# Output banks that alternate between groups, first loads in another order, and three copies done by DMA, in an attention and MLP kernel

## The chip, the cores and the metric

One core of a Trainium2 chip runs the kernel. The number is device time in microseconds, median of several runs. Before the change it is 1764.37 us, the median of three runs (1763.39 to 1766.12).

## The reference

Agent attention for 4 batches of 12,480 tokens with 49 agents, and then a two-layer MLP with squared ReLU on all 49,920 tokens:

```python
def sm(a, b):
    s = scale * (a @ b.transpose(0, 2, 1))
    s = s - s.max(-1, keepdims=True)
    e = np.exp(s)
    return e / (e.sum(-1, keepdims=True) + 1e-09)
agent_v = sm(agents, k) @ v          # 49 x 128 per batch
x = sm(q, agents) @ agent_v          # 49,920 x 128
h = x @ w_in                         # 128 x 2048
r = np.maximum(h, 0.0)
out = (r * r) @ w_out                # 2048 x 128
```

The inputs are float32; the weights come in as 64-bit floats and are turned into 32-bit floats on the chip.

## The kernel before, in words

**Tiles and groups.** The tokens are cut into 52 groups of 960 tokens, 13 to a batch. For a group, the 2048 hidden units are 16 tiles of 128. Tile i of the whole run goes through: `mm1` (six matmuls from the softmax rows `p_a`, `p_b` and the folded weights `w_a`, `w_b` into a PSUM tile `h`), `relu` and `square` on ACT (tile `g`), `high` (`gh`, g rounded to the fast matmul type, by a casting DMA from the POOL queue or by DVE), `low` on DVE (`gl` = g - gh), and `mm2` (twelve matmuls that add gh x wo_hi, gh x wo_lo and gl x wo_hi into the output sums `out`). A value and its rounding error are kept as two tiles of the fast type everywhere: p_a and p_b, w_a and w_b, wo_hi and wo_lo, gh and gl.

**What else a group needs.** The softmax rows of two groups at a time are made by `q_scores` (PE), `q_turn`, `q_max`, `q_sub`, `q_total`, `q_norm`, `q_back` (DVE), `q_exp` (ACT), `q_spread` (DMAs on SP into `pt`), `q_hi` (L382, ACT: p_a is the rounded pt) and `q_lo` (DVE: p_b = pt - p_a). For the next batch the keys and values come in seven sets: `k_scores` (PE), `k_copy` (ACT, into `sk`), `k_max` (DVE), after the last set `k_bias` (the maximum over all keys, through PE and DVE, into `mb`), then `k_exp` (ACT), `k_turn` (DVE, into `pe`), `v_acc` (PE) and `v_sum` (DVE), `a_final`, and `w_make`, which folds the result into `w_in`. The text calls the pieces of PE work among these insertions.

**The order.** Each engine gets its work in the order of a list `steps` sorted by a time counted in tiles. At time i stand mm1 and relu of tile i and mm2 of tile i - 8 (`LAG`), two tiles' mm2 at a time. `chain` finds free times for an insertion and its followers on ACT and DVE; `hop` is the distance between them. The end of group s is at time 16s + 23, where ACT and DVE copy the two output banks to `ob` (`store_a`, `store_d`, L454 and L458) and SP stores it.

**PSUM.** Eight banks: two `h` tiles of two banks (`ps_h`), the output sums of one group (`ps_o`, two banks), and one two-bank tile for insertions (`ps_a`). The first mm2 of a group writes the banks that the stores of the group before read. So `plan_queries` and `plan_keys` put scores at the ends of groups (time `boundary(s)`), and `early_mm1` puts two mm1 of the next tiles ahead of the first mm2.

**Start.** Batch 0 has no work to hide behind: scores of its first queries and of seven sets of keys, the bias, then seven sets of values into one PSUM bank, `a_first`, `w_first`, and the conversion of weights from 64-bit floats (`to_f32`, five DVE instructions and one ACT instruction for each of four blocks of w_in, `win_make`, and of w_out, `wo_make`; L85 to L90). Blocks of w_out then give `wo_hi` (L111, ACT) and `wo_lo` (L113, POOL). Short matmuls on zeros (`warm_up`) fill some of PE's gaps. Value tiles `vt` of the start come from a pool of six buffers shared with later loads, so the seventh load waits until PE has used the first.

**Turn of row tiles.** Matmuls of mm2 use half the array's rows each. Where the half that writes a bank changes, PE waits for a no-operation on POOL's queue (`relay`, L437), which itself waits for the matmul before.

Of the kernel before, what the change touches and what calls it, by code (L numbers as in the profile page):

```python
# [27 lines left out]
def agent_attention_relu2_kernel(ctx: ExitStack, tc: tile.TileContext, qT, kT, v, agT, w_in, w_out, outT):  # L28
# [24 lines left out]
    ps_o = ctx.enter_context(tc.tile_pool(name="ps_o", bufs=1, space=bass.MemoryType.PSUM))  # L53
    ps_a = ctx.enter_context(tc.tile_pool(name="ps_a", bufs=1, space=bass.MemoryType.PSUM))
# [19 lines left out]
    def raw_load(t, src):  # L74
        raws[t, src is wi_bits] = raw = ew.tile([P, PW, 2], U32, name="raw", tag="gl", bufs=LB)
        nc.sync.dma_start(out=raw, in_=src[:, t * PW:(t + 1) * PW, :])

    def to_f32(raw, dst):
# [3 lines left out]
        x = ew.tile([P, PW], F32, name="cv_x", tag="gh", bufs=HB)  # L82
# [34 lines left out]
    sk = cpool.tile([P, NP, 2, KW], F32, name="sk")  # L117
# [13 lines left out]
    turn = [0]  # L131
# [3 lines left out]

    def att():
        return ps_a.tile([P, 2, 512], F32, name="ps_att")

    def pair_of_banks():

        turn[0] += 1
        return new_h() if many[0] and turn[0] % 3 else att()
# [285 lines left out]
    def mm2(i, turn, first=False, last=False):  # L428
# [3 lines left out]
        if first:  # L432
            outs[s] = [ps_o.tile([P, 512], F32, name=f"out{t}") for t in range(2)]
# [48 lines left out]
    KEYS = (14, 17, 20, 32, 34, 36)  # L482
# [7 lines left out]
    def at(t, f, *args):  # L490
# [5 lines left out]
           "DVE": {"PE": 2, "ACT": 2, "DVE": 1, "POOL": 3}, "POOL": {"PE": 1, "ACT": 4, "DVE": 4, "POOL": 1}}  # L496
    taken = {(e, s * NF + NF - 1 + LAG) for s in range(NSG) for e in ("ACT", "DVE")}
    kept = {(e, s * NF + NF - 1 + LAG - x) for s in range(NSG) for e, n in (("ACT", 3), ("DVE", 2)) for x in range(n)}
    taken |= {("PE", s * NF + NF - 1 + LAG) for s in range(NSG - 3)}
    banks = set()  # L500

    def chain(t, todo):
# [4 lines left out]
        while todo:  # L507
# [24 lines left out]
    urgent = (k_copy, k_max, k_bias, a_final)  # L532
    reads_bank = (k_copy, k_max, k_bias, v_sum, a_final, w_make, q_turn)

    def boundary(s):
        return s * NF + NF - 1 + LAG

    def free_from(g, *engines):
        while any((e, g) in taken for e in engines):
            g += 1  # L540
        taken.update((e, g) for e in engines)
        return g
# [3 lines left out]
    def plan_queries(u):  # L546

        t = boundary(2 * u - 4)
        g = free_from(t + 1, "DVE")
        banks.update(range(t, g + 2))  # L550
        for x, s in enumerate(members(u)):
            at(t - LEAD + .1 * x, q_load, s)
        at(t + .005, q_scores, u)
        at(g + .5, q_turn, u)
        return u, g + (2 if u > 2 else 1)

    def plan_rows(u, g):
        todo = [("DVE", q_max, u), ("DVE", q_sub, u), ("ACT", q_exp, u), ("DVE", q_total, u), ("DVE", q_norm, u), ("DVE", q_back, u)]
        for e, f, _ in todo:
            _, t = chain(g, [(e, f, u)])  # L560
            g = t + (2 if u > 2 or f is q_exp else 1)
# [8 lines left out]
    def k_loads(b, n, t):  # L570
        for x in range(2):
            at(t + .01 * x, k_load, b, 2 * n + x)

    def plan_keys(b, n, s):

        t = boundary(s)
        g = free_from(t + 1, "DVE", "ACT")
        banks.update(range(t, g + 2))
        if t > 40:
            k_loads(b, n, t - LEAD)  # L580
        at(t + .005, k_scores, b, n)
        at(g + .5, k_copy, n)
        at(g + .52, k_max, n)
        return g + 1
# [5 lines left out]
    def plan_values(b, t0, stop):  # L590
# [3 lines left out]
        for n in range(NP):  # L594
            _, t1 = chain(max(t0 + 1 + int(n * d), used.get(n - 2, 0)), [("ACT", k_exp, n), ("DVE", k_turn, n)])
            turned[b, n] = t1
# [3 lines left out]
        _, end = chain(end + 2, [("PE", a_final, 0), ("DVE", a_final, 1), ("DVE", a_final, 2)])  # L600
# [3 lines left out]

    turned, keyed = {}, {}
# [5 lines left out]
    vps = [ps_o.tile([P, 512], F32, name=f"out{t}") for t in range(2)]  # L611
# [9 lines left out]
    order, t = {}, 5.0  # L621
    queue = [("q", 0, 1.75)]
    for n in range(NP):
        queue += [("k", n, 1.75), ("w", 1, .65)]
    queue += [("b", 1, .5), ("w", 2, .5), ("b", 3, .5), ("w", 4, 1.6)]
    for x in range(2 * NP):
        queue.append(("v", x, 1.2))
# [8 lines left out]
    for x, t in ((7, 0), (12, 1), (18, 2)):  # L636
        loads.insert(x, (raw_load, t, wi_bits))
    loads += [(raw_load, 3, wi_bits), (raw_load, 0, wo_bits), (q_load, 1), (q_load, 2), (raw_load, 1, wo_bits), (raw_load, 2, wo_bits), (raw_load, 3, wo_bits), *((k_load, 1, n) for n in range(4))]
    t = 0
    for n, (f, *args) in enumerate(loads):  # L640
        if f is v_load and args[1] >= 6:
            t = order["v", args[1] - 6] + 1.2
        at(Z + t + .001 * n, f, *args)
    at(Z, warm_up, 1, 0)
# [21 lines left out]
    t = last
    at(Z + t + .05, a_first, 0)
# [19 lines left out]
    banks.update([*range(9), *(x + y for x in KEYS for y in range(3))])  # L687
# [4 lines left out]
    taken.update((e, t) for e in ("ACT", "DVE") for x in KEYS for t in (x, x + 1) if t < 30 or t == x)  # L692
    taken.update((("ACT", 5), ("DVE", 6), ("ACT", 7), ("DVE", 8)))
    plan_halves(1, 12)
    for n, t in enumerate((3.2, 14.1, 20.1, 23.1, 30.1), 2):
        k_loads(1, n, t)
    for n, t in enumerate(KEYS):
        at(t + .02, k_scores, 1, n)
        at(t + .5, k_copy, n)
        at(t + .52, k_max, n)  # L700
# [3 lines left out]
    rows = [plan_queries(u) for u in range(2, NSG // 2 + 1)]  # L704
    ends = {1: plan_keys(1, NP - 1, 1)}
    for b in range(2, B):
        for n in range(NP):
            s = 14 * b - 25 + 2 * n
            ends[b] = plan_keys(b, n, s)
            keyed[b, n] = boundary(s)  # L710
    for u, g in rows:
        plan_rows(u, g)
    for b in range(1, B):
        plan_values(b, plan_bias(ends[b] + 1), b * NS * NF)
    for b, n in keyed:
        assert turned[b - 1, n] + 1 < keyed[b, n], (b, n, turned[b - 1, n], keyed[b, n])
# [68 lines left out]
```

## Time and profile before

| | |
|---|---|
| median of three runs | 1764.37 us |
| the profiled execution's own time | 1766.49 us |
| its span, first to last instruction | 1764.6 us |
| PE busy | 1731.9 us (98%) |
| ACT busy | 1622.1 us (92%) |
| DVE busy | 1458.8 us (83%) |
| POOL busy | 245.8 us (14%) |
| mean granted TensorE clock | 0.994 of full speed |

The profile is one execution. Times in its rows are microseconds from its first instruction. Matmuls overlap, so a row's duration is longer than the distance to the next. "Idle before" is the time for which an engine did nothing ahead of an instruction, with the event that ended the wait. A POOL or SP row of a DMA is the issue alone; "to landing" counts from there to the last byte.

### The profile page before, as it was taken

What the parts mean: (1) busy time and instruction counts of PE and PEld (TensorE: products, weight loads), DVE (VectorE), ACT (ScalarE), POOL (GpSimd) and SP (SyncE); (2) the same over time, 40 slices, a digit from 0 to 9 for tenths busy, and PEclk for the clock granted to TensorE, in tenths of its full rate; (3) what the DMA queues carried; (4) which work ended last, traced back from release to release, by engine and by line L of the source; (5) the groups of instructions that cost most, each with busy time, mean ns of one, the idle gap of its engine ahead of it and who ended that gap; (6) DMA issues with size and microseconds to landing.
All of it is one profiled execution on the core that took longest, in us unless ns stands there. A gap on an engine that the chain in (4) does not pass through costs nothing.

```text
span 1764.6 us, 41495 instructions
## 1 busy us (share of the span) xinstructions
PE 1731.9 (98%) x16835; PEld 1498.5 (85%) x16839; DVE 1458.8 (83%) x1740; ACT 1622.1 (92%) x1909; POOL 245.8 (14%) x453
## 2 busy tenths in 40 slices
PE   8799999999999999999999999999999999999998
PEld 3477888888988888888888888888889888988897
DVE  5767888988978878888988888878887898898887
ACT  4588999999999989999999999999999999999997
POOL 0122111111111111111111111111111111111110
PEclk8999999999999999999999999999999999999999
DMA  8888565465455565565454555565545535544542
GB/s 294 300 307 290 188 222 198 166 217 186 163 182 176 172 210 187 177 229 192 159 198 161 177 187 190 174 214 189 175 161 168 186 140 181 178 163 163 180 148 105
DMA packets 105728, 337.80 MB, mean 191 GB/s; under 512 B 13952, under 2 KB 20864, under 8 KB 105536
## 3 DMA queue, kind: packets, MB, share of 16 engines
q0 software_dynamic: 63200, 215.56, 34.7%
q1 hardware_dynamic: 42336, 119.59, 20.8%
q8 instruction: 132, 2.16, 0.5%
q14 instruction: 60, 0.49, 0.1%
HBM read 81.47 MB, written 25.56 MB: 61 GB/s over the span
## 4 chain that ended last, share of the span: by engine, by line
PE 87%; DMA 4%; DVE 3%; ACT 3%; issue 2%; POOL 0%; DVEq 0%; POOLq 0%; ACTq 0%
PE out L442 52%; PE h L408 26%; PE ps_att L164 4%; DMA gh<-g 3%; PE ps_att L227 2%; DVE gl L426 1%; ACT g L412 1%; ACT g L415 1%; DVE mxs L182 1%; PE ps_att L307 1%; PE out L227 1%; PE out L615 0%; DMA qt<-qT 0%; ACT sk L179 0%; DMA vt<-v 0%
## 5 line engine op out<-in xcount | busy, mean ns | idle before, releaser
L426 DVE TENSOR_TENSOR gl<-g,gh 128x960 fp32r<-128x960 f32 x832 | 923.6, 1150 | 117.2 <-DMA gh<-g 110.4
L412 ACT ACTIVATE g<-h 128x960 f32<-128x960 f32 x832 | 818.6, 984 | 83.9 <-PE h L408 83.2
L415 ACT ACTIVATE g<-g 128x960 f32<-128x960 f32 x832 | 846.4, 1017 | 0.0
L442 PE MATMUL out<-gh,wo_hi 64*128 64x480 f32 x3328 | 620.4, 368 | 6.4 <-ACT wo_hi L111 3.2
L442 PE MATMUL out<-gl,wo_hi 64*128 64x480 f32 x3328 | 613.2, 364 | 2.7 <-DVE gl L426 2.5
L442 PE MATMUL out<-gh,wo_lo 64*128 64x480 f32 x3328 | 611.0, 362 | 1.1 <-POOL wo_lo L113 1.1
L420 POOL DMA_DIRECT2D gh<-g x438 | 237.3, 542 | 1476.2 <-ACT g L415 568.4
L442 PEld LDWEIGHTS out<-gh,wo_hi 64*128 64x128 f32 x3328 | 315.8, 185 | 44.6 <-issue 8.3
L442 PEld LDWEIGHTS out<-gl,wo_hi 64*128 64x128 f32 x3328 | 316.2, 185 | 31.3 <-DVE gl L426 8.6
L442 PEld LDWEIGHTS out<-gh,wo_lo 64*128 64x128 f32 x3328 | 318.8, 187 | 23.0 <-POOL wo_lo L113 1.4
L408 PE MATMUL h<-p_a,w_a 49*128 49x480 f32 x1664 | 315.2, 374 | 0.8 <-ACT w_a L291 0.4
L408 PE MATMUL h<-p_a,w_b 49*128 49x480 f32 x1664 | 305.2, 362 | 0.0
L408 PE MATMUL h<-p_b,w_a 49*128 49x480 f32 x1664 | 304.7, 362 | 0.0
L422 DVE CAST gh<-g 128x960 fp32r<-128x960 f32 x394 | 257.4, 653 | 5.1 <-ACT g L415 4.2
L408 PEld LDWEIGHTS h<-p_a,w_a 49*128 49x128 f32 x1664 | 158.9, 186 | 47.1 <-ACT ob L454 26.0
L408 PEld LDWEIGHTS h<-p_b,w_a 49*128 49x128 f32 x1664 | 160.2, 188 | 10.2
L408 PEld LDWEIGHTS h<-p_a,w_b 49*128 49x128 f32 x1664 | 157.2, 184 | 12.5
L458 DVE COPY ob<-out 128x480 f32<-128x480 f32 x52 | 34.2, 657 | 78.4 <-PE out L442 78.2
L182 DVE TENSOR_REDUCE mxs<-ps_att 128x2 f32<-128x896 f32 x23 | 25.0, 1089 | 56.4 <-ACT sk L179 56.4
L164 PE MATMUL ps_att<-qt,ag_sb 128*32 128x480 f32 x408 | 47.2, 572 | 0.0
L210 DVE STREAM_TRANSPOSE pe<-sk 128x896 f32<-128x896 f32 x28 | 31.0, 1106 | 14.1 <-ACT sk L206 9.1
L454 ACT COPY ob<-out 128x480 f32<-128x480 f32 x52 | 30.0, 577 | 10.8 <-PE out L442 10.8
(88 smaller groups left out, 642.8 us busy)
## 6 DMA issues: line engine op xcount, KB each, us to landing
gh<-g POOLq DMA_DIRECT2D x438, 480.0 KB, 3.0
vt<-v SPq DMA_DIRECT2D x56, 451.5 KB, 5.8
kt<-kT SPq DMA_DIRECT2D x56, 448.0 KB, 5.1
qt<-qT SPq DMA_DIRECT2D x52, 480.0 KB, 6.6
outT<-ob SPq DMA_DIRECT2D x51, 480.0 KB, 3.1
pt<-et SPq DMA_DIRECT2D x204, 60.0 KB, 2.8
raw<-w_in SPq DMA_DIRECT2D x4, 512.0 KB, 9.5
raw<-w_out SPq DMA_DIRECT2D x4, 512.0 KB, 10.6
```

The lines of the kernel that those rows point to most:

```text
L164: nc.tensor.matmul(ps[32 * j:32 * j + 32, h, :w], ags[j // 2][:, 32 * h:32 * h + 32], xs[j // 2][:, j % 2 * w:j % 2 * w + w], start=True, ...
L182: nc.vector.tensor_reduce(out=mx[:, n], in_=pss.pop(("k", n))[:, :, :KW], axis=AX.X, op=ALU.max)
L210: nc.vector.transpose(squares(pes[n]), sk[:, n].rearrange("p h (b c) -> p h b c", c=32))
L227: nc.tensor.matmul(ps[t:t + A, :C + 1], pes[n][:, c, :A], vt[:, y, :], start=n == first and c < 2, stop=n == last and c >= KC - 2)
L408: nc.tensor.matmul(hs[i][:, t, :TT], w, two(p), start=n == 0, stop=n == 2)
L412: nc.scalar.activation(gs[i], hs.pop(i)[:, :, :TT], AF.Relu)
L415: nc.scalar.activation(gs[i], gs[i], AF.Square)
L420: nc.gpsimd.dma_start(out=ghs[i], in_=gs[i])
L422: nc.vector.tensor_copy(ghs[i], gs[i])
L426: nc.vector.tensor_tensor(out=gls[i], in0=gs.pop(i), in1=ghs[i].bitcast(F32), op=ALU.subtract)
L442: mm = nc.tensor.matmul(o[u][:, :TT], w[rows, j, :], two(g[rows, u, :]), start=first and n == 0, stop=last and n == 2)
L458: nc.vector.tensor_copy(ob_of(s)[:, 1, :], outs[s][1][:, :TT])
```

## The change: what it does

Three things. `ps_o` and `ps_a` become one pool of two pairs of banks: group s sums into pair s % 2, and insertions use the other pair. The planner no longer puts scores at the ends of groups; it puts them inside, nowhere within the three times from a group's end, and mm1 is no longer moved ahead. All scores of the start now use the two h tiles alone (before, every third used `ps_a`).

`q_hi` and the rounding of w_out into `wo_hi` are casting DMAs on POOL's queue instead of ACT copies.

At the start, all keys are loaded ahead of the first block of w_in; eight of the fourteen value tiles use buffers of `gh`, which no longer makes them wait for PE; three blocks of w_out are loaded into a part of `sk`; conversions of w_in move from the key scores to the values; the first two blocks of w_out are converted earlier. Keys of batch 1 are scored from time 26 on instead of from 14.

```diff
-    ps_o = ctx.enter_context(tc.tile_pool(name="ps_o", bufs=1, space=bass.MemoryType.PSUM))
-    ps_a = ctx.enter_context(tc.tile_pool(name="ps_a", bufs=1, space=bass.MemoryType.PSUM))
+    pairs = ctx.enter_context(tc.tile_pool(name="pairs", bufs=1, space=bass.MemoryType.PSUM))
...
+        raw = ew.tile([P, PW, 2], U32, name="raw", tag="gl", bufs=LB) if src is wi_bits or t == 0 else sk_bits[:, t - 1]
...
-            nc.scalar.copy(wo_hi[:, sl, :], f)
+            nc.gpsimd.dma_start(out=wo_hi[:, sl, :], in_=f)
...
+    def pair(n, name):
+        return pairs.tile([P, 2, 512], F32, name=name, tag=f"pair{n % 2}")
+
     def att():
-        return ps_a.tile([P, 2, 512], F32, name="ps_att")
+        return pair(group[0] + 1, "ps_att")
...
-        vts[x] = io.tile([P, VC, C + 1], F32, name="vt", tag="io")
+        vts[x] = io.tile([P, VC, C + 1], F32, name="vt", tag="io") if b or x < 6 else ew.tile([P, VC, C + 1], F32, name="vt", tag="gh", bufs=HB)
...
-        nc.scalar.copy(PT[s][0][:M], pts[s][:M])
+        nc.gpsimd.dma_start(out=PT[s][0][:M], in_=pts[s][:M])
...
-            outs[s] = [ps_o.tile([P, 512], F32, name=f"out{t}") for t in range(2)]
+            group[0] = s
+            o = pair(s, "out")
+            outs[s] = [o[:, t] for t in range(2)]
...
+    banks = {s * NF + NF - 1 + LAG + x for s in range(NSG) for x in range(3)}
...
-            _, t = chain(max(t, s * NF - 9 if s > 1 else 0), [("ACT", q_hi, s), ("DVE", q_lo, s)])
+            _, t = chain(max(t, s * NF - 9 if s > 1 else 0), [("POOL", q_hi, s), ("DVE", q_lo, s)])
...
-    for x, t in ((7, 0), (12, 1), (18, 2)):
+    for x, t in ((15, 0), (16, 1)):
         loads.insert(x, (raw_load, t, wi_bits))
...
-    early_mm1 = {s * NF + NF + LAG + x: s * NF + NF - 1 + LAG + x + .02 for s in range(NSG - 3) for x in range(2)}
```

On PE, at the end of a group in the middle of the run, the row of instructions before is this (out0_11808 and out1_11809 are the sums of the group that ends, out0_12278 and out1_12279 those of the next, in the same banks; ps_att is the insertion's tile):

```order
L442 MATMUL out0_11808<-gl_12136,wo_hi_88 128x480
L442 MATMUL out1_11809<-gl_12136,wo_hi_88 128x480
L164 MATMUL ps_att_12244<-kt_12025,ag_sb_76 32x448 x2
L164 MATMUL ps_att_12244<-kt_12039,ag_sb_76 32x448 x2
L164 MATMUL ps_att_12244<-kt_12025,ag_sb_76 32x448 x2
L164 MATMUL ps_att_12244<-kt_12039,ag_sb_76 32x448 x2
L408 MATMUL h_12253<-p_a_11834,w_a1_6653 128x480 x2
L408 MATMUL h_12253<-p_b_11835,w_a1_6653 128x480 x2
L408 MATMUL h_12253<-p_a_11834,w_b1_6654 128x480 x2
L408 MATMUL h_12260<-p_a_11834,w_a2_6738 128x480 x2
L442 MATMUL out0_12278<-gh_12129,wo_hi_88 128x480
L442 MATMUL out1_12279<-gh_12129,wo_hi_88 128x480
```

The same end of a group in the changed kernel (out_11856 ends, out_12326 begins, in the other pair; L411 is mm1 and L447 is mm2):

```order
L447 MATMUL out_11856<-gh_12158,wo_hi_85 128x480 x2
L447 MATMUL out_11856<-gh_12158,wo_lo_86 128x480 x2
L447 MATMUL out_11856<-gl_12209,wo_hi_85 128x480 x2
L411 MATMUL h_12305<-p_a_11853,w_a1_6683 128x480 x2
L411 MATMUL h_12305<-p_b_11854,w_a1_6683 128x480 x2
L411 MATMUL h_12305<-p_a_11853,w_b1_6684 128x480 x2
L447 MATMUL out_12326<-gh_12202,wo_hi_85 128x480 x2
L447 MATMUL out_12326<-gh_12202,wo_lo_86 128x480 x2
```

The scores and one mm1 have left the place between the last mm2 of a group and the first of the next.

On DVE, the rows around the key scores of the start before (L182 is k_max, L385 is q_lo of group 0, L187 is the first step of k_bias, L85 to L90 convert w_in):

```order
L89 SCALAR_TENSOR_TENSOR cv_p<-raw,cv_p 128x512
L385 TENSOR_TENSOR p_b<-pt,p_a 113x480
L182 TENSOR_REDUCE mxs<-h 128x2
L90 SCALAR_TENSOR_TENSOR win_sb<-cv_x,cv_p 128x512
L182 TENSOR_REDUCE mxs<-h 128x2
L187 TENSOR_REDUCE mp<-mxs 128x2
```

The same place in the changed kernel (L185 is k_max, L388 is q_lo, L205 writes mb, the last step of k_bias, L213 is k_turn):

```order
L185 TENSOR_REDUCE mxs<-h 128x2 x5
L190 TENSOR_REDUCE mp<-mxs 128x2
L199 TENSOR_REDUCE mt<-ps_att 2x32
L200 COPY mt<-mt 2x96
L388 TENSOR_TENSOR p_b<-pt,p_a 113x480
L205 TENSOR_SCALAR mb<-ps_att 128x2
L85 TENSOR_SCALAR cv_p<-raw 128x512
L87 TENSOR_SCALAR cv_x<-raw 128x512
L88 SCALAR_TENSOR_TENSOR cv_x<-raw,cv_x 128x512
L213 STREAM_TRANSPOSE pe<-sk 128x2x14x32
```

The conversions have gone from among the maxima, and q_lo, which reads the p_a that is now a DMA's, stands right ahead of the instruction that ends the bias.

On POOL's queue, the first groups in the changed kernel (L381 spreads group 0's softmax rows, L385 is q_hi, L111 makes wo_hi, L423 is high, L113 makes wo_lo):

```order
L381 DMA pt<-et 32x480 x4
L385 DMA p_a<-pt 113x480
L111 DMA wo_hi<-wo_f 128x512
L423 DMA gh<-g 128x960
L113 TENSOR_TENSOR wo_lo<-wo_f,wo_hi 128x512
L111 DMA wo_hi<-wo_f 128x512
L423 DMA gh<-g 128x960 x2
L113 TENSOR_TENSOR wo_lo<-wo_f,wo_hi 128x512
L423 DMA gh<-g 128x960 x6
L111 DMA wo_hi<-wo_f 128x512
L385 DMA p_a<-pt 113x480
```

Before, this queue held the spread, the casts of g and the four subtractions alone. Now each subtraction follows a cast on the same queue whose landing it waits for.

## Rows read from the trace of the kernel before

**Rows 1.** Busy time by stretch: span, each engine, PEclk, DMA share, GB/s.

```profile
0.00:57.00 57.00, 45.98 (x360) 23.03 (x363) 31.70 (x51) 18.86 (x28) 2.99 (x11) 0.91 0.85 313
57.00:100.00 43.00, 36.25 (x267) 23.70 (x270) 33.53 (x47) 35.86 (x46) 11.14 (x16) 0.92 0.76 261
100.00:170.00 70.00, 67.60 (x644) 52.72 (x640) 48.49 (x51) 60.48 (x71) 17.43 (x31) 1.00 0.91 305
170.00:1700.00 1530.00, 1523.20 (x15002) 1345.84 (x15004) 1298.18 (x1542) 1454.52 (x1707) 207.91 (x383) 1.00 0.54 182
```

**Rows 2.** Groups by line and shape: busy us, mean ns, idle before us.

```profile
L442 PE MATMUL out<-gh,wo_hi 64*128 64x480 f32 x3328 | 620.4, 368 | 6.4 <-ACT wo_hi L111 3.2 <-ACT ob L454 2.3
L113 POOL TENSOR_TENSOR wo_lo<-wo_f,wo_hi 128x512 fp32r<-128x512 f32 x4 | 5.6, 1405 | 6.9 <-ACT wo_hi L111 6.9
L210 DVE STREAM_TRANSPOSE pe<-sk 128x896 f32<-128x896 f32 x28 | 31.0, 1106 | 14.1 <-ACT sk L206 9.1 <-PE out L227 2.3 <-issue 1.5
```

**Rows 3.** Timeline of the start, keys: start us, us, instruction [idle before].

```profile
25.54 0.59 ACT L382 CAST p_a<-pt 113x480 fp32r<-113x480 f32 x1 [0.53 <-DMA pt<-et]
27.71 0.65 DVE L385 TENSOR_TENSOR p_b<-pt,p_a 113x480 fp32r<-113x480 f32 x1
30.99 0.17 DVE L187 TENSOR_REDUCE mp<-mxs 128x2 f32<-128x14 f32 x1
33.41 0.16 DVE L202 TENSOR_SCALAR mb<-ps_att 128x2 f32<-128x2 f32 x1 [0.93 <-PE ps_att L200]
```

**Rows 4.** Landing: pt at the start, gh from 57 to 72, all gh.

```profile
DMA to landing us min/median/max: 6.5/6.6/6.6
...
DMA to landing us min/median/max: 4.6/5.2/6.1
...
DMA to landing us min/median/max: 2.8/3.0/8.9
```

**Rows 5.** Timeline of the start, values, on PE and DVE.

```profile
36.09 8.78 PE L227 MATMUL out<-vt,pe 128*49 128x129 f32 x112 [0.90 <-DVE pe L210]
47.60 5.59 PE L227 MATMUL out<-vt,pe 128*49 128x129 f32 x70 [0.76 <-DMA vt<-v]
53.23 0.29 DVE L241 COPY acc<-out 113x129 f32<-113x129 f32 x1 [3.34 <-PE out L227]
```

**Rows 6.** Chain of waits: one set of values in the steady part.

```profile
302.91 1.68 PE ps_att L227 x28
```

**Rows 7.** Timeline of DVE where the first differences gl are made.

```profile
60.36 0.69 DVE L90 SCALAR_TENSOR_TENSOR win_sb<-cv_x,cv_p 128x512 f32<-128x512 f32 x1
61.57 0.42 DVE L85 TENSOR_SCALAR cv_p<-raw 128x512 uint32<-128x512 uint32 x1
65.80 1.18 DVE L341 STREAM_TRANSPOSE e<-ps_att 128x960 f32<-128x960 f32 x1 [1.42 <-PE ps_att L164]
67.73 1.16 DVE L426 TENSOR_TENSOR gl<-g,gh 128x960 fp32r<-128x960 f32 x1 [0.74 <-DMA gh<-g]
```

**Rows 8.** PE in group 0; busy time of two stretches.

```profile
84.94 0.47 PE L442 MATMUL out<-gh,wo_hi 64*128 64x480 f32 x2 [3.18 <-ACT wo_hi L111]
86.48 0.77 PE L442 MATMUL out<-gh,wo_lo 64*128 64x480 f32 x2 [1.07 <-POOL wo_lo L113]
...
35.00:40.00 5.00, 4.10 (x39) 3.86 (x40) 2.70 (x3) 3.25 (x6) 0.00 (x0) 0.50 0.17 44
85.00:92.50 7.50, 6.43 (x34) 5.20 (x36) 5.88 (x8) 5.26 (x7) 2.53 (x3) 0.54 0.52 166
```

**Rows 9.** A late cast: POOL, DVE, then busy time by stretch.

```profile
618.89 0.53 POOL L420 DMA_DIRECT2D gh<-g  x1 [5.11 <-PE h L408]
627.21 2.23 DVE L426 TENSOR_TENSOR gl<-g,gh 128x960 fp32r<-128x960 f32 x2 [2.52 <-DMA gh<-g]
...
626.00:631.50 5.50, 4.37 (x40) 3.10 (x36) 4.25 (x7) 4.94 (x7) 1.06 (x2) 1.00 0.54 194
631.50:635.00 3.50, 3.50 (x19) 3.02 (x20) 3.50 (x6) 0.98 (x2) 0.00 (x0) 0.51 0.42 145
```

More of the change, by code (lines that the diff above doesn't have):

```diff
@@ L481, in agent_attention_relu2_kernel @@
     SKIP = (7, 12)
-    KEYS = (14, 17, 20, 32, 34, 36)
     FROM = 0
@@ L515, in chain @@
                     g += hop[p][e] if p else 0
-                    while (e, g) in taken or f not in urgent and (e, g) in kept:
+                    while (e, g) in taken:
                         g += 1
@@ L530, in chain @@
         return first, t
-    urgent = (k_copy, k_max, k_bias, a_final)
     reads_bank = (k_copy, k_max, k_bias, v_sum, a_final, w_make, q_turn)
[L535 to L542, printed above, removed]
     LEAD = 7
     def plan_queries(u):
-        t = boundary(2 * u - 4)
-        g = free_from(t + 1, "DVE")
-        banks.update(range(t, g + 2))
+        first, t = chain(32 * u - 46, [("PE", q_scores, u), ("DVE", q_turn, u)])
         for x, s in enumerate(members(u)):
[L552 to L555, printed above, removed]
+            at(first - LEAD + .1 * x, q_load, s)
+        plan_rows(u, t + 2)
     def plan_rows(u, g):
@@ L566, in plan_halves, with plan_keys @@
         for s in members(u):
-            _, t = chain(max(t, s * NF - 9 if s > 1 else 0), [("ACT", q_hi, s), ("DVE", q_lo, s)])
+            _, t = chain(max(t, s * NF - 9 if s > 1 else 0), [("POOL", q_hi, s), ("DVE", q_lo, s)])
             assert t + 1 < s * NF, (s, t)
-    def k_loads(b, n, t):
+    def plan_keys(b, n, t):
+        first, end = chain(t, [("PE", k_scores, b, n), ("ACT", k_copy, n), ("DVE", k_max, n)])
         for x in range(2):
[L572 to L584, printed above, removed]
+            if b > 1 or n > 1:
+                at(first - LEAD + .1 * x, k_load, b, 2 * n + x)
+        return end
     def plan_bias(t):
@@ L599, in plan_values @@
                 at(used[n] - LEAD + .1 * x, v_load, b, 2 * n + x)
-        _, end = chain(end + 2, [("PE", a_final, 0), ("DVE", a_final, 1), ("DVE", a_final, 2)])
+            if b < B - 1:
+                keys = plan_keys(b + 1, n, t1 + 6)
+        last, end = chain(end + 2, [("PE", a_final, 0), ("DVE", a_final, 1), ("DVE", a_final, 2)])
         for f in range(F // 512):
@@ L603, in plan_values @@
             assert end + 2 < stop + 4 * f, (b, f, end, stop)
-    turned, keyed = {}, {}
+        if b < B - 1:
+            return max(last + 2, plan_bias(keys + 1))
     warm = wk.tile([P, 512], BF16, name="warm", tag="ob", bufs=1)
     nc.vector.memset(warm, 0.0)
-    vps = [ps_o.tile([P, 512], F32, name=f"out{t}") for t in range(2)]
+    vps = pair(0, "out")
+    vps = [vps[:, t] for t in range(2)]
     def warm_up(n, t):
@@ L703, in agent_attention_relu2_kernel @@
             at(t + y, w_make, 0, f, x)
[L704 to L712, printed above, removed]
+    for u in range(2, NSG // 2 + 1):
+        plan_queries(u)
+    end = 22
+    for n in range(NP):
+        end = plan_keys(1, n, end + 3)
+    ready = plan_bias(end + 1)
     for b in range(1, B):
-        plan_values(b, plan_bias(ends[b] + 1), b * NS * NF)
-    for b, n in keyed:
-        assert turned[b - 1, n] + 1 < keyed[b, n], (b, n, turned[b - 1, n], keyed[b, n])
-    early_mm1 = {s * NF + NF + LAG + x: s * NF + NF - 1 + LAG + x + .02 for s in range(NSG - 3) for x in range(2)}
+        ready = plan_values(b, ready, b * NS * NF)
     for i in range(NG):
         late = i in SKIP or i < NF + LAG and (i < LAG or (i - LAG) % NF == 0)
-        at(early_mm1.get(i, i if late else i + .01), mm1, i)
-        at(i + (.035 if i + 1 in early_mm1 and i not in early_mm1 else .1), relu, i)
+        at(i if late else i + .01, mm1, i)
+        at(i + .1, relu, i)
         at(i + 1.2, square, i)
```

72 lines of the change are left out of this document (33 added, 39 removed).

## The prediction

> **What bounds the kernel now.** I read the busy time by stretch first. From 170 to 1700 us PE is busy for 1523.2 of 1530.0 us at full clock, while ACT has 1454.5 and DVE 1298.2 [rows 1]. So nine tenths of the span are PE's own matmuls, which the change neither removes nor adds: 6.8 us of idle time is all that can be won there. The rest of PE's idle time is early: 11.0 us before 57, 6.8 from 57 to 100, 2.4 from 100 to 170, with clock below full in the first two [rows 1]. The change therefore has to be priced in the start and in group 0, and for the long middle the question is only whether it brings new stalls. I went on to the groups by line, for what PE waited for, and then to the timeline of the start.
>
> **The ends of groups.** In the middle, the first mm2 of a group could wait for the stores of the group before, since both use the same banks. The rows put 2.3 us in total on PE waiting for the output copy (L454), because scores and an early mm1 stand in between [rows 2]. With two pairs that wait has no cause left: the next group writes banks whose stores ended a group earlier, and the insertions that share that pair stay away from the group's end. I take -2.3 us. The ends are 0 (the wait turns into one for something else) and -6.8, all idle time of that stretch. Moving the scores inward costs nothing by itself: the same matmuls in the same number, and the copies that follow them on ACT and DVE have the slack of rows 1 as cover. If that cover were gone, ACT's spare 75 us over 1530 would have to be lost first.
>
> **The copies that leave ACT.** 52 copies of 0.59 us [rows 3] are 31 us of ACT time, but ACT is not the bound in any long stretch, so I count 0 (at best -1). What they become matters more: 52 casts and four more on POOL's queue, each waiting in order.
>
> **The start, keys.** In the trace, conversions stood among the key maxima (five DVE instructions a block, two of 0.42 and three of 0.69 us, so 2.9 a block [rows 7]), and the bias began at 30.99 and ended at 33.57 [rows 3]. With all keys loaded first and two blocks of conversions gone, the maxima can end some 5 us earlier. But DVE now has q_lo of group 0 right ahead of the instruction that ends the bias, and q_lo needs the cast of p_a. The spread softmax rows had landed by 25.5, when ACT began its copy [rows 3]; nothing ahead of them changes much. So the cast is issued at about 25.5. How long does it take? No such cast is in the trace. The nearest rows: 6.5 to 6.6 us for the small spread DMAs at that very time, 5.2 (median) for casts of g between 57 and 72, when the DMA engines were as busy, and 2.8 to 8.9 over all casts [rows 4]. I take 5.2 to 6.6, the two busy ones: landing at 30.7 to 32.1, plus 0.65 for q_lo and 0.16 for the bias [rows 3], so 31.5 to 32.9 instead of 33.57. That is -0.7 to -2.1; I take -1.3. With 2.8 it would be 29.1, so -4.5; with 8.9, 35.2, so +1.6. Behind the waiting q_lo on DVE stand the conversions and all k_turn, and PE's value matmuls wait for those.
>
> **The start, values.** Four sets of value matmuls ran from 36.09 to 44.87, then PE waited for loads, and the sum was copied at 53.23 [rows 5]. Eight value tiles now have buffers of their own and need not wait for PE. Then three sets remain: PE needs 1.68 each [rows 6], DVE 1.11 for the transpose [rows 2] and at most 0.69 for a conversion between [rows 7], so 1.8. 44.87 + 3 x 1.8 = 50.3, which is -2.9. The first sets ran at the half level of the clock (1.2 GHz, 0.50 from 35 to 40 [rows 8]) after PE had waited, and PE will have waited there again. The ends: 0, if PE stays at half clock through the later sets (3 x 1.68 more eats it), and -5.4, if it is at full clock from the beginning (2.5 us of the 5).
>
> **Conversions that move later.** Three instructions of a block (1.5 us) now stand on DVE between the copy of the value sum and the reciprocal; part of that lies beside PE's matmuls on the sum, so I take +0.6 (0 to 1.5). Ahead of the first difference gl DVE has one more block, 2.9 us, against 1.42 + 0.74 = 2.16 us in which it was idle there [rows 7]: +0.75 (0 to 2.9). Together +1.35.
>
> **Group 0.** The fifth tile's mm2 waited 3.18 us for wo_hi and 1.07 us for wo_lo, because block 1 of w_out was converted late. Behind the wait the clock was at its lower level: 0.54 over 85.0 to 92.5 [rows 8], where 0.46 x 7.5 = 3.4 us are missing, about 2.8 of them not in idle time. So 4.25 + 2.8 = 7.0 us were lost. The change converts block 1 before the first gl, and this stall goes. What is late next? Blocks 2 and 3: from DVE's last conversion, POOL issues the cast of wo_hi, waits for its landing (3.0, median [rows 4]) and subtracts (1.4 [rows 2]): 0.5 + 3.0 + 1.4 = 4.9 us in which its queue stands. Behind it stand the casts of g, but also the no-operations for which PE waits at each turn of row tiles. PE has 1.8 us of work in a tile (six and twelve matmuls) before the next turn: 4.9 - 1.8 = 3.1 for block 2, and for block 3, which comes two tiles later when PE is already late, I add 0.4. That is 3.5 instead of 7.0: -3.5. The ends: all 7.0 won (DVE finishes the blocks ahead of PE), or none (both blocks cost 3.1 and the clock falls again).
>
> **Casts on the DMA engines.** From 100 to 170 their share is already 0.91 and PE lost 2.4 us [rows 1]; all casts of g go by DMA there. The new casts are small and key loads move later into this stretch: +1 (0 to 5).
>
> **Sum.** -2.3 - 1.3 - 2.9 + 1.35 - 3.5 + 1 = -7.65 us. The profiled execution took 1766.49, so 1758.8; it lies 2.1 us above the median of the runs, 1764.37, which becomes 1756.7. I say 1757.
>
> **Rivals.** *The cast is quick* (0.12). If p_a lands as the quickest casts did, in 2.8 us [rows 4], the bias ends at 29.1 and the start wins 3.2 us more: 1753.5. For it: the DMA is half the size of a cast of g. Against: the spread DMAs of the same moment, 32 of its 113 rows each, took 6.5. The Trainium skill ("DMA: Bandwidth & Descriptors", section on the anatomy of one DMA on the gpsimd path) gives 2.0 us plus the bytes over 436 GB/s for a DMA from this queue, so 2.5 us for these 217 KB by an estimate from that page; by that rule this rival would be the forecast, but the spread rows disagree with it by 4 us when the engines are full.
>
> *The gains are handed back* (0.21). The cast lands in 8.9 us (+2.9 against my 1.3), and POOL's waits in group 0 cost PE 7.0 again with a fall of the clock (+3.5): -1.25, so 1763. For it: the engines are full at that time, and three producers now share POOL's queue. Against: 8.9 is the longest landing of all casts, and the median is a third of it.
>
> *Late casts in the middle, slower* (0.17). At 618.89 a cast of g met a bunch of loads and landed 8.3 us later; DVE waited 2.52, PE was idle for 5.50 - 4.37 = 1.13 us and then ran 3.5 us at half level (0.51), 1.75 lost: 2.9 us an event [rows 9]. The kernel before has one such event. If the casts of p_a, in line with those of g, and loads for insertions that now follow each other closer make five more, it is +14.5 - 7.65 = +6.9, so 1771. It decides from four on. Against: the median landing of 3.0 with a share of 0.54 [rows 1, 4].
>
> That the pairs change nothing at the ends is possible too; it costs 2.3 and stays in the forecast's own range, 1753 to 1761.
>
> **Chances.** The forecast has 0.50. Differences under 0.2% (3.5 us) can't be told from none here, so faster means below 1760.8 and slower above 1767.9. Faster: 0.45 of the forecast's 0.50 and the first rival's 0.12, 0.57. Same: 0.05, the second rival's 0.20 and 0.01 of the third: 0.26. Slower: the third's other 0.16 and 0.01 of the second: 0.17. The range 1749 to 1768 leaves 0.05 below (both unknowns of the start at their good ends) and 0.15 above.
>
> **What would show it.** Right: q_lo of group 0 waits on DVE for a DMA, with mb at 31.5 to 33; the value sum copied at about 49; no wait of PE for wo_hi, but waits for POOL's no-operations in group 0; no wait for L454's successor in the groups' first mm2; idle time of PE from 170 on at 4 to 7 us. Wrong: mb before 30 or after 34; a fall of the clock in group 0; more than one stretch at the lower level after 170; ACT ahead of PE's mm1 as what it waits for.

## The result and the profile after

The changed kernel takes 1783.87 us (median of 4 runs, 1782.12 to 1789.64) against 1764.84 for the kernel before (4 runs): the ratio is 1.0114, with an interval of 1.0089 to 1.0138. It is slower by 1.1%, where 0.4% faster was predicted.

The busy time by stretch of the changed kernel, with the columns of [rows 1] (span, PE, PEld, DVE, ACT, POOL with counts, granted clock, DMA share, GB/s):

```profile
0.00:57.00 57.00, 45.24 (x377) 22.94 (x377) 33.10 (x55) 20.71 (x31) 3.54 (x12) 0.91 0.98 369
57.00:100.00 43.00, 35.91 (x268) 23.99 (x268) 37.77 (x47) 35.12 (x42) 15.55 (x23) 0.92 0.69 225
100.00:170.00 70.00, 69.53 (x666) 55.36 (x664) 47.20 (x48) 61.75 (x71) 18.70 (x36) 1.00 0.95 320
170.00:1700.00 1530.00, 1508.60 (x14786) 1323.39 (x14786) 1274.92 (x1518) 1418.62 (x1633) 235.59 (x420) 1.00 0.57 187
```

The counts of matmuls say where the time went. The kernel before did 360 + 267 + 644 = 1271 up to 170 us and 15,002 from there to 1700 [rows 1]; the changed one did 1311 and 14,786. A matmul stands for 1523.2 / 15,002 = 0.1015 us there, so the start is some 4 us ahead (a little less, as some of the 40 are warm-up) and the long middle is behind by 216 x 0.1015 = 21.9 us. The middle is the stretch in which I had looked for no more than 6.8 us of idle time to win.

What PE waited for in the middle (170 to 1700 us: total, times, longest), the five largest rows of the changed kernel:

```profile
PE ps_att L310 <- DVE w_b L321: 6.7, 3, 2.9
PE out L447 <- DVE gl L429: 6.7, 21, 0.5
PE ps_att L261 <- DVE mxs L185: 4.0, 2, 2.5
PE out L447 <- DMA gh<-g: 1.8, 3, 0.8
PE ps_att L230 <- DVE mxs L185: 1.6, 1, 1.6
```

All but one row have DVE as what ended the wait, and L310, L261 and L230 are insertions (w_make, a_final, values). DVE itself was busy for 83% of that time, so the question is what DVE was waiting for. Two of its groups, over the whole run:

```profile
L429 DVE TENSOR_TENSOR gl<-g,gh 128x960 fp32r<-128x960 f32 x832 | 922.6, 1148 | 139.4 <-DMA gh<-g 134.5 <-PE out L447 3.9
L463 DVE COPY ob<-out 128x480 f32<-128x480 f32 x52 | 34.2, 658 | 108.1 <-ACT ob L459 108.1
```

The answering rows of before:

```profile
L426 DVE TENSOR_TENSOR gl<-g,gh 128x960 fp32r<-128x960 f32 x832 | 923.6, 1150 | 117.2 <-DMA gh<-g 110.4 <-PE out L442 3.2 <-PE h L408 1.5
L458 DVE COPY ob<-out 128x480 f32<-128x480 f32 x52 | 34.2, 657 | 78.4 <-PE out L442 78.2
```

Both waits grew: DVE stands longer at casts that land late, and its output copy now waits for ACT's in every group. From the timeline of DVE I counted its waits of over 2 us for a cast from group 3 on ("late casts" in what follows): 18 before, 25 now, and all 25 are for a tile 6 of its group. The casts themselves say the same: from issue to landing those of tiles 6 took 5.2 us at the median before and take 6.9 now (49 casts from group 3 on), while those of tiles 2 and 4 stay near 3. One late cast, in the timeline around 510 us:

```profile
498.54 0.55 POOL L385 DMA_DIRECT2D p_a<-pt  x1
...
500.61 0.35 SPq L477 DMA_DIRECT2D outT<-ob  x1
501.05 1.17 SPq L335 DMA_DIRECT2D qt<-qT  x2
...
501.94 0.53 POOL L423 DMA_DIRECT2D gh<-g  x1 [2.86 <-PE out L447]
...
502.32 0.93 SPq L219 DMA_DIRECT2D vt<-v  x2
...
510.05 2.23 DVE L429 TENSOR_TENSOR gl<-g,gh 128x960 fp32r<-128x960 f32 x2 [3.50 <-DMA gh<-g]
...
512.76 0.68 DVE L321 TENSOR_TENSOR w_b<-ps_att,w_a 113x512 fp32r<-113x512 f32 x1
...
513.50 0.69 PE L310 MATMUL ps_att<-win_sb,a 64*113 64x256 f32 x4 [2.93 <-DVE w_b L321]
```

Read it from the top: within some four microseconds a cast of p_a, the output store, two query loads, a cast of g and two value loads are asked for. That cast of g, issued at 501.94, is the one of tile 6; it landed at 510.02, 8.1 us later. The cast of p_a had landed by 501.98, so what is under way beside the late cast is the store and the loads, those just ahead of it and those just behind. DVE needs its result and stands for 3.50 us. Behind DVE's row stands w_b, which frees the insertions' banks, and PE needs those for the next w_make, so PE stands as well. Then the clock falls (span, busy times and granted clock of the two stretches):

```profile
508.00:514.00 6.00, 3.07 (x32) 2.52 (x28) 3.95 (x5) 3.26 (x4) 0.00 (x0) 1.00 0.67 247
514.00:519.00 5.00, 5.00 (x36) 4.40 (x35) 3.94 (x6) 2.56 (x4) 1.06 (x2) 0.66 0.28 98
```

PE does 32 matmuls in 6 us, and 36 in the 5 us after it. At 0.1015 us each, these 11 us hold 6.9 us of work: 4.1 us lost. From 170 us on the clock was at half level three times (443.4 to 446.8, 515.0 to 518.5, 1361.5 to 1368.4); the kernel before had one such stretch [rows 9].

### The profile page after: what moved, and what is told of

Same layout as the page of the kernel before. It is cut to its first block, busy times and chain, and to the rows that moved or that the text cites. A ratio compares the mean times of both kernels' runs of the same rounds, so it can differ in the third digit from the quotient of the medians.

```text
span 1781.5 us, 41424 instructions
## 1 busy us (share of the span) xinstructions
PE 1736.2 (97%) x16841; PEld 1496.3 (84%) x16841; DVE 1457.4 (82%) x1740; ACT 1606.2 (90%) x1853; POOL 283.7 (16%) x509
## 4 chain that ended last, share of the span: by engine, by line
PE 80%; DMA 9%; DVE 4%; issue 3%; ACT 3%; POOL 0%; POOLq 0%; DVEq 0%; ACTq 0%
PE out L447 48%; PE h L411 24%; DMA gh<-g 9%; PE ps_att L167 4%; PE ps_att L230 2%; DVE gl L429 2%; ACT g L418 2%; ACT g L415 1%; PE out L230 1%; PE ps_att L310 1%; PE out L597 0%; DMA p_a<-pt 0%; DMA pt<-et 0%; DVE mxs L185 0%; DVE gh L425 0%
## 5 line engine op out<-in xcount | busy, mean ns | idle before, releaser
L429 DVE TENSOR_TENSOR gl<-g,gh 128x960 fp32r<-128x960 f32 x832 | 922.6, 1148 | 139.4 <-DMA gh<-g 134.5
L447 PE MATMUL out<-gh,wo_hi 64*128 64x480 f32 x3328 | 623.4, 371 | 5.3 <-POOLq L442 3.1
L447 PE MATMUL out<-gl,wo_hi 64*128 64x480 f32 x3328 | 613.3, 365 | 7.3 <-DVE gl L429 6.9
L447 PE MATMUL out<-gh,wo_lo 64*128 64x480 f32 x3328 | 609.4, 363 | 0.0
L423 POOL DMA_DIRECT2D gh<-g x438 | 245.2, 560 | 1404.8 <-ACT g L418 482.9
L447 PEld LDWEIGHTS out<-gh,wo_hi 64*128 64x128 f32 x3328 | 314.0, 185 | 72.9 <-issue 38.9
L447 PEld LDWEIGHTS out<-gl,wo_hi 64*128 64x128 f32 x3328 | 314.5, 186 | 42.2 <-DVE gl L429 18.5
L447 PEld LDWEIGHTS out<-gh,wo_lo 64*128 64x128 f32 x3328 | 317.2, 187 | 22.0
L411 PE MATMUL h<-p_a,w_a 49*128 49x480 f32 x1664 | 310.9, 370 | 0.4 <-ACT w_a L294 0.4
L411 PE MATMUL h<-p_b,w_a 49*128 49x480 f32 x1664 | 304.2, 362 | 1.0 <-DVE p_b L388 1.0
L411 PE MATMUL h<-p_a,w_b 49*128 49x480 f32 x1664 | 304.6, 363 | 0.0
L411 PEld LDWEIGHTS h<-p_a,w_a 49*128 49x128 f32 x1664 | 158.3, 187 | 16.4 <-ACT g L415 1.4
L411 PEld LDWEIGHTS h<-p_b,w_a 49*128 49x128 f32 x1664 | 159.8, 189 | 12.5 <-DVE p_b L388 1.4
L411 PEld LDWEIGHTS h<-p_a,w_b 49*128 49x128 f32 x1664 | 156.4, 184 | 13.0
L344 DVE STREAM_TRANSPOSE e<-ps_att 128x960 f32<-128x960 f32 (+1 forms) x26 | 30.7, 1182 | 34.9 <-PE ps_att L167 34.9
L209 ACT ACTIVATE sk<-sk,mb 128x448 f32<-128x448 f32 x56 | 33.9, 665 | 8.6 <-DVE mb L205 8.6
L230 PE MATMUL ps_att<-vt,pe 128*49 128x129 f32 x588 | 36.7, 275 | 2.1 <-DVE mxs L185 1.6
## 6 DMA issues: line engine op xcount, KB each, us to landing
raw<-w_in SPq DMA_DIRECT2D x4, 512.0 KB, 10.9
```

The lines of the kernel that those rows point to most:

```text
L209: nc.scalar.activation(sk[:, n, h], sk[:, n, h], AF.Exp, bias=mb[:, h:h + 1], scale=scale)
L230: nc.tensor.matmul(ps[t:t + A, :C + 1], pes[n][:, c, :A], vt[:, y, :], start=n == first and c < 2, stop=n == last and c >= KC - 2)
L344: nc.vector.transpose(squares(es[u]), pss.pop(("q", u))[r, :, :TT].rearrange("p h (b c) -> p h b c", c=32))
L411: nc.tensor.matmul(hs[i][:, t, :TT], w, two(p), start=n == 0, stop=n == 2)
L423: nc.gpsimd.dma_start(out=ghs[i], in_=gs[i])
L429: nc.vector.tensor_tensor(out=gls[i], in0=gs.pop(i), in1=ghs[i].bitcast(F32), op=ALU.subtract)
```

## The experiments

The theories are named in the expectations: L (late casts of tile 6 hold DVE's queue), S (the two output copies one behind the other), C (the new casts of p_a crowd the casts of g), P (the insertions stand too close). Each ratio is to the kernel before on the same chip. Differences in us between two kernels are of their medians, which were not all taken on one chip; the kernel before took 1761.60 to 1764.84 us beside them, so such a difference can be off by some 3 us.

**e1, the kernel before with one out tile.**

```diff
-            outs[s] = [ps_o.tile([P, 512], F32, name=f"out{t}") for t in range(2)]
+            o = ps_o.tile([P, 2, 512], F32, name="out")
+            outs[s] = [o[:, t] for t in range(2)]
```

> The kernel before, with the two output banks of a group as one tile of the program, as in the changed kernel; nothing else. In the trace of the changed kernel DVE's copy of the second bank waits for ACT's copy of the first in all 52 groups, before it waited for PE. Theory S (this wait makes DVE late and is the loss): 1773 to 1785. Theories L (late casts of the tile 6 hold DVE's queue), C (the casts of p_a crowd the casts of g) and P (the insertions stand too close): within 3 us of 1764.8.

Measured 1778.01 us, ratio 1.0081 (1.0059 to 1.0104). DVE's output copy waits for ACT's in all 52 groups here too, and PE's first matmul of a group now waits for DVE's copy (groups by line, e1):

```profile
L459 DVE COPY ob<-out 128x480 f32<-128x480 f32 x52 | 34.2, 657 | 127.6 <-ACT ob L455 127.6
L443 PE MATMUL out<-gh,wo_hi 64*128 64x480 f32 x3328 | 619.4, 368 | 14.8 <-DVE ob L459 10.9 <-ACT wo_hi L111 3.2
```

So two copies from one tile of the program run one behind the other, and with one pair of banks that costs 15.6 us. The order is the program's own: in e1 and in the changed kernel all 52 of DVE's copies wait for the semaphore that ACT's copy raises, before none did, and 50 of 52 ran beside ACT's. But the way of the loss is another than in the changed kernel: PE waits 10.9 us for the copy itself, a row that is absent there, and the late casts are 16.

**e2, the changed kernel with q_hi on ACT.**

```diff
-        nc.gpsimd.dma_start(out=PT[s][0][:M], in_=pts[s][:M])
+        if s:
+            nc.scalar.copy(PT[s][0][:M], pts[s][:M])
+        else:
+            nc.gpsimd.dma_start(out=PT[s][0][:M], in_=pts[s][:M])
...
-[("POOL", q_hi, s), ("DVE", q_lo, s)]
+[("ACT", q_hi, s), ("DVE", q_lo, s)]
```

> The changed kernel with q_hi back on ACT for all groups but group 0, planned as an ACT step. Theory C: most of the 19 us come back, 1764 to 1770, and casts of tile 6 land earlier than the 8.0 us from issue to gl. Theories L, S and P: 1780 to 1787; ACT's 30 us more are not on the path.

Measured 1774.43 us, 1.0066 (1.0051 to 1.0081): 9.4 us of the 19 come back (7.0 when each kernel is measured against the kernel before on its own chip), between the two expectations. DVE's wait for casts of g goes from 134.5 to 117.3 us, the median landing of tiles 6 from 6.9 to 5.8 us, and of the 25 late casts 21 stay. The casts of p_a are one reason of the lateness and not the only one.

**e3, casts of tiles 6 by DVE.**

```diff
-        return FROM <= i < NG - 4 and (i % 2 == 0 or i < 3 * NF)
+        return FROM <= i < NG - 4 and (i % 2 == 0 and i % NF != 6 or i < 3 * NF)
```

> The changed kernel with the cast of every tile 6 of a group done by DVE (0.65 us) instead of POOL's queue, from group 3 on. Theory L: the 25 waits of over 2 us for a cast go, and with them PE's waits for the maxima and for w_b and the three falls of the clock: 1762 to 1769. Theories S and P: PE's waits stay, 1778 to 1786. Theory C: the lateness moves to tile 8, 1778 to 1786.

Measured 1750.04 us, 0.9929 (0.9915 to 0.9944): 33.8 us less than the changed kernel (31.4 when each is measured against the kernel before on its own chip), and 12.4 less than the kernel before. The gain is larger than theory L had said. The middle of the run by busy time, and then all that PE waits for in it:

```profile
170.00:1700.00 1530.00, 1528.13 (x15122) 1352.84 (x15120) 1331.16 (x1601) 1451.36 (x1672) 217.34 (x383) 1.00 0.52 175
```

```profile
PE ps_att L310 <- DVE w_b L321: 1.3, 1, 1.3
PE out L447 <- DVE gl L429: 0.5, 2, 0.3
```

PE does 15,122 - 14,786 = 336 matmuls more in the same 1530 us, 34.1 us of work, which is the whole gain. Late casts are 4, and the clock does not fall in this stretch.

**e9, the control: tiles 12 instead of 6.** The line of e3 with `i % NF != 12`.

> Control for e3: the changed kernel with the casts of tiles 12 of a group, not 6, on DVE; the same number of casts leaves the DMA engines and the same number comes to DVE. Theory L (it is the cast behind the stores and loads that counts): 1778 to 1787, 20 or more waits of over 2 us left. Theory C' (any 49 casts fewer on the DMA engines would do): 1750 to 1762.

Measured 1787.39 us, 1.0140 (1.0123 to 1.0156), 27 late casts, 26 of them for a tile 6. As many casts left the DMA engines (48 against 49), as many came to DVE, and nothing was won. It is this one cast, not their number.

**e4, q_lo of group 0 later.**

```diff
-(q_back, 5.4), (q_hi, 11), (q_lo, 17)):
+(q_back, 5.4), (q_hi, 11)):
         at(Z + t + y, f, 0)
+    at(Z + order["t", 3] + .005, q_lo, 0)
```

> The changed kernel with q_lo of group 0 moved on DVE from ahead of the end of the bias to between the value transposes. If the wait for the cast of p_a (landed 7.0 us after its issue) is what held the start: mb at about 28.7 us instead of 33.8, the values up to 5 us earlier, 1778.5 to 1781. If the value loads bound the values anyway: 1783 to 1785. Theories L, S, C and P say nothing on it: the middle stays as it is.

Measured 1781.85 us (1777.97 to 1788.58), 1.0114 (1.0086 to 1.0141): 2 us less than the changed kernel, less than these runs scatter, with the same ratio; it lies between the two expectations. The trace shows the start itself clearly (timeline of e4):

```profile
28.04 0.16 DVE L205 TENSOR_SCALAR mb<-ps_att 128x2 f32<-128x2 f32 x1 [0.53 <-PE ps_att L203]
...
44.86 0.29 DVE L244 COPY acc<-out 113x129 f32<-113x129 f32 x1 [3.51 <-PE out L230]
```

The bias ends 5.6 us earlier than in the changed kernel and the value sum is copied 4.7 us earlier. The wait for the cast of p_a had held both. How much of this is left at the end of the run, these medians do not show.

**e5, the kernel before with tiles 6 cast by DVE** (the line of e3).

> The kernel before with the casts of tiles 6 of a group on DVE, as e3 did it to the changed kernel. Theory L1 (late casts cost before little, since nothing that PE waits for stands behind them on DVE): 1759 to 1763, a gain of 0 to 4. Theory L2 (they cost the kernel before as much an event, and only come more often after the change): 18 of 25 events, so up to 12 us less, 1750 to 1755.

Measured 1759.05 us, 0.9970 (0.9959 to 0.9981): 3.7 us less, so theory L1. The kernel before pays 3.7 us for its 18 late casts, the changed one 33.8 for 25, some 1.4 us each.

**e6, the changed kernel with the edits of e3 and e4.**

> The changed kernel with both edits: casts of tiles 6 on DVE (e3) and q_lo of group 0 behind the end of the bias (e4). If the two are independent, the 4.9 us that e4's trace had won at 100 us, of which 3.1 were left at 170, come off e3's 1750.0: 1745 to 1748. If the start's gain is lost again in the filling of the pipeline: 1749 to 1751.

Measured 1746.09 us, 0.9897 (0.9882 to 0.9912), inside the first expectation: the fastest of all, 1.0% faster than the kernel before.

**e7, both banks copied by one ACT instruction.**

```diff
-        nc.scalar.copy(ob_of(s)[:, 0, :], outs[s][0][:, :TT])
+        if s < NSG - 1:
+            nc.scalar.copy(ob_of(s), full.pop(s)[:, :, :TT])
```

> The changed kernel with one ACT instruction copying both banks of a group's sums (for all groups but the last); DVE's copy, which waited for ACT's in all 52 groups, is gone. Theory S (DVE's wait at a group's end makes its next differences and maxima late, here as in e1): 6 to 15 us back, 1768 to 1778. Theory L (two pairs leave the stores a whole group's time, so that wait costs nothing itself): 1780 to 1786, DVE's waits for casts of tile 6 as many as before the edit.

Measured 1804.47 us, 1.0227 (1.0209 to 1.0244): outside both expectations. The copy takes ACT 0.95 us in place of about 0.55, ahead of squares that the next casts need:

```profile
L461 ACT COPY ob<-out x51: 946/951/1092, 115.6 to 1772.8; 128x960 f32<-128x960 f32 x51
```

DVE's wait for casts rises from 134.5 to 204.9 us and its waits of over 2 us ahead of a gl to 38 (29 of them put down to a cast). But the casts of tiles 6 land no later: in 6.4 us at the median, against 6.9 in the changed kernel. DVE comes to them earlier, since its own copy and the wait for ACT's are gone, and so it stands longer: how long an engine stands does not say how late a transfer is. Which part of the edit costs the 20.6 us is not shown; some 0.4 us more of ACT in each group is one candidate. What DVE's wait for ACT's copy costs in the changed kernel can be read from e3 instead, where it is as long as ever,

```profile
L463 DVE COPY ob<-out 128x480 f32<-128x480 f32 x52 | 34.2, 658 | 108.5 <-ACT ob L459 108.5
```

while all that PE waits for in the middle is 1.8 us. With the late casts gone this wait costs next to nothing; whether it adds to the price of a late cast was not tested.

**e8, query loads earlier.**

```diff
-            at(first - LEAD + .1 * x, q_load, s)
+            at(first - 12 + .1 * x, q_load, s)
```

> The changed kernel with the loads of queries asked for 12 times ahead of the scores instead of 7, so that on SP's queue they stand ahead of the output store and no longer right behind it. If the bunch of output store, two query loads and two value loads is what delays the cast of tile 6: fewer than 12 waits of over 2 us instead of 25, and 1765 to 1775. If the lateness comes from POOL's queue or from the place of the cast in the group: 1780 to 1787, 20 waits or more.

Measured 1769.25 us, 1.0041 (1.0026 to 1.0056), 14.6 us less; 18 late casts, 12 of them for a tile 6. The time is in the first expectation and the count is not: taking two query loads out of the bunch helps (tiles 6 land in 4.3 us at the median instead of 6.9), but moves some lateness to tiles 2 and 4.

**e12, e2 and e8 together.**

> The changed kernel with the edits of e2 (q_hi on ACT) and e8 (query loads ahead of the store) together, the casts of tiles 6 left on POOL's queue. If they are two separate reasons for one lateness, 9.5 and 14.6 us add up: 1758 to 1764. If either is enough: 1767 to 1771. If lateness stays at other tiles: above 1771.

Measured 1767.84 us, 1.0032 (1.0020 to 1.0044), 12 late casts: 1.4 us below e8 alone, inside the second expectation. The two do not add up, as two parts of one crowd would not.

**e13, gl of tiles 6 later on DVE.**

```diff
-            at(i + 5.2, low, i)
+            at(i + (6.8 if i % NF == 6 and i >= 3 * NF else 5.2), low, i)
```

> The changed kernel with gl of every tile 6 (from group 3 on) moved back on DVE by 1.6 times of the plan, so that what stood behind it there goes first; the cast itself stays on POOL's queue, with the same loads beside it. Theory L (DVE standing at the late cast is what costs): PE's 12.8 us of waits for maxima and w_b go to under 4, 1758 to 1772. If the late cast costs by its own mm2, since gl of tile 6 is needed: 1780 to 1790, and PE's waits for gl, 6.7 us, rise above 12.

Measured 1767.35 us, 1.0015 (1.0004 to 1.0027). All that PE waits for in the middle:

```profile
PE out L447 <- DVE gl L429: 7.6, 13, 1.6
PE out L447 <- DMA gh<-g: 2.7, 3, 1.2
```

The waits of insertions, 12.3 us in the rows of the changed kernel above, are gone altogether, and 16.5 us come back with the cast as late as before (tiles 6 land in 6.7 us at the median, 6.9 without the edit): this half went by way of DVE's queue. The other half, 17.3 us to e3, is shown in part: PE's waits for gl and gh in the middle are 10.3 us here and 0.5 in e3. The rest is not accounted for.

**e14, insertions kept away from a group's end for five times** (`range(3)` becomes `range(5)` in the line of `banks`).

> The changed kernel with insertions kept away from a group's end for five times instead of three, so that fewer of them have their DVE step behind the cast of tile 6; that cast is untouched. If the price of a late cast depends on what stands behind it on DVE: 20 late casts or more, but PE's waits for maxima and w_b under 8 us instead of 12.8, 1768 to 1779. If the place of the insertions doesn't matter: 1780 to 1788.

Measured 1784.16 us, 1.0118 (1.0101 to 1.0135), inside the second expectation. In its trace PE's waits for maxima and w_b do fall, from 12.3 to 7.7 us, but the late casts rise to 31; that trace is of the fastest execution, 1776.64 us. In the median nothing is won.

**e10 and e11, e6 with q_hi on ACT and e6 with the earlier query loads.**

> e6 (casts of tiles 6 on DVE, q_lo of group 0 later) with q_hi on ACT for all groups but group 0. If the casts of p_a cost only by making the cast of tile 6 later: within 3 us of 1746, 1743 to 1749. If they cost by themselves, as in e2: 1736 to 1742. If ACT's 51 more copies cost, since ACT's delay at a group's end cost 20 us in e7: 1750 to 1760.

> e6 with the query loads asked for 12 times ahead, as in e8. With the cast of tile 6 gone from the queue the bunch has little to delay: within 3 us of 1746. If earlier loads only move the lateness to another cast (in e8 it stood at tiles 2 and 4 five times): 1748 to 1756.

Measured 1748.18 us, 0.9919 (0.9904 to 0.9934), and 1755.49 us, 0.9963 (0.9949 to 0.9977). Once the cast of tile 6 has left the queue, the casts of p_a cost no more than ACT's copies (e10 is 2.1 us above e6), and earlier loads cost 9.4 us: in e11 the late casts are few (3), and the loss is early: from 100 to 300 us it does 1876 matmuls where e6 does 1944, 68 x 0.1015 = 6.9 us. Why the earlier loads cost there was not followed further.

## Why the prediction was wrong, step by step

**The step that failed** is the term for casts on the DMA engines, +1 us with 0 to 5 as its ends, together with the price of the third rival. It was taken from the stretch from 100 to 170, and there nothing was lost: 666 matmuls were done against 644. The loss is in the middle, where I had put "the question is only whether it brings new stalls" and then weighed one event, 2.9 us [rows 9]. The third rival named the right mechanism, with its place and sign, at a chance of 0.17 and with five events for 1771. There were 25, and the result lies 13 us past that rival's own time. By e3 they cost 33.8 us, by e5 those of before 3.7: a term of about +30 us stood at +1. I had counted one event before, the one with a fall of the clock, and put in five more at 2.9 us each. By DVE's waits there were 18 before and seven more now; what changed most is what one costs, from 0.2 to 1.4 us, and for that the rival had nothing. The page of before held the warning: DVE waited 110.4 us for casts. I read that as idle time of an engine that is not the bound, and asked how long a cast takes at the median (3.0 us [rows 4]). I should have asked which cast is issued among the store and the loads, how late it is, and what stands behind it on DVE.

With it failed "moving the scores inward costs nothing by itself", which rested on idle time of ACT and DVE as cover. Of the 12.3 us for which PE's insertions wait in the middle, 5.6 are for mxs, the maxima of the key scores that were moved, and e13 shows that such waits go when DVE does not stand at the late cast ahead of them. Idle time on average was no cover behind one long wait.

**The copies that leave ACT**, counted at 0: by e2 they cost 9.4 us as DMAs, and the cast of tile 6, which each precedes on POOL's queue, lands later with them. How they delay it is not shown: in the event above the cast of p_a had landed as the late one was issued. I had named that risk in words and given it no term in the middle. With the cast of tile 6 gone (e10) the 0 holds within some 3 us.

**The ends of groups**, -2.3: PE's wait for the output copy has gone from the profile, as predicted; the row of the first mm2 now has POOL's no-operations in group 0 as its largest releaser:

```profile
L447 PE MATMUL out<-gh,wo_hi 64*128 64x480 f32 x3328 | 623.4, 371 | 5.3 <-POOLq L442 3.1 <-DMA gh<-g 1.8
```

**Keys**, -1.3: nothing was won. In place of [rows 3] the timeline of the changed kernel has

```profile
26.05 0.54 POOL L385 DMA_DIRECT2D p_a<-pt  x1 [6.92 <-DMA pt<-et]
...
33.06 0.66 DVE L388 TENSOR_TENSOR p_b<-pt,p_a 113x480 fp32r<-113x480 f32 x1 [5.47 <-DMA p_a<-pt]
33.63 0.15 DVE L205 TENSOR_SCALAR mb<-ps_att 128x2 f32<-128x2 f32 x1
...
49.56 0.29 DVE L244 COPY acc<-out 113x129 f32<-113x129 f32 x1 [1.28 <-PE out L230]
```

The mechanism was right (q_lo waits on DVE for the cast, and the bias behind it), and the size was 6.9 us for the landing where I took 5.2 to 6.6. The neighbouring spread DMAs with their 6.5 were the better guide. By the rule of the Trainium skill ("DMA: Bandwidth & Descriptors", anatomy of one DMA on the gpsimd path) the estimate was 2.5 us; the trace disagrees, with 6.9 here and 3.5 at the median later.

**Values and conversions**: the value sum was copied 3.7 us earlier where -1.3 and -2.9 make 4.2, and the first mm1 came at 53.8 instead of 56.95 us. The first gl came at 67.24 against 67.73 [rows 7], so 2.7 of those 3.2 us went to conversions that now stand ahead of it, where I had +0.75.

**Group 0**, -3.5: the wait for wo_hi and wo_lo is gone, and PE waited 3.1 us for POOL's no-operations, close to the 3.5 worked out; but it did so four times, 1.1 us at most, where I had one wait of 3.1 and one of 0.4, so the agreement is in part luck. But a wait I had not seen came ahead of it (timeline of PE, then the busy time of the stretch behind it):

```profile
67.37 0.73 PE L310 MATMUL ps_att<-win_sb,a 64*113 64x256 f32 x4 [2.50 <-DVE e L344]
```

```profile
67.50:75.00 7.50, 7.28 (x31) 3.96 (x33) 6.63 (x7) 3.95 (x5) 2.50 (x4) 0.54 0.50 168
```

q_turn, which empties the insertions' banks, stands on DVE behind the same conversions, and after PE's wait the granted clock is 0.54 again. From 57 to 100 us there are 268 matmuls against 267: the stall was exchanged for another. In e3, e9 and e13, whose start is the same program, this stretch has 273, 254 and 241 matmuls, so one execution says only that nothing large was won.

**The sum without the failed step.** With tiles 6 cast by DVE in both kernels, e3 and e5, the change is worth 1750.04 - 1759.05 = -9.0 us, near the -7.65 of the sum. The parts come out about right together and not one by one: keys and group 0 gave nothing where I had -4.8, and the middle does 15,122 matmuls in e3 against 15,076 in e5, 4.7 us of work, where I had -2.3. That the total fits is in part luck. The late casts, which cost 33.8 us now and 3.7 before, take 30 us the other way.

**What stays open.** The kernel before has 110 us of DVE waiting for casts, and e2, with 117, loses 14,864 against 15,002 matmuls in the middle; so the same waiting costs more after the change. e13 shows that half of the loss passes through what stands behind the cast on DVE, e14 that moving insertions by two times does not help. Which placement of the insertions makes it cheap in the kernel before was not settled. Two things on record bear on it, and no run tried them. The change also drops the rule `kept`, by which insertions that were not urgent stayed off ACT for three times and off DVE for two up to a group's end. And DVE's lead over PE is shorter ahead of the late cast: from the end of gl of a tile 2 to the first matmul that reads it are 4.5 us at the median before and 1.6 after (groups 3 to 49).

## What to carry to other kernels

Idle time of an engine off the bound costs nothing only while nothing that the bound needs stands behind the wait: for an in-order engine list what is queued behind its longest wait, and ask whether the change puts something there. When a transfer is added or moved, price the one cast or load that will travel in the crowd, not the median one; which tile that is can be read from the order of the queues, and taking only that tile off the queue was worth 34 us here. And always run the control with another tile of the same number.

## What the runs showed that I had not expected

Two copies on two engines that read different banks of one tile of the program run one behind the other (52 of 52 in the changed kernel and in e1), by a semaphore that the program waits for, while from two tiles they ran side by side; in the kernel before this alone cost 15.6 us. One copy of both banks by ACT, in place of two, cost 20.6 us, and which part of it does so is open (e7). A cast of 212 KB took 6.9 us with the DMA engines full at the start, and 3.5 at the median later.
